# The last V block with two stationary quarters, and half a block of wo in eleven transfers of six partitions

## The chip, the core and the metric

The kernel runs on one core of a Trainium2 chip. The core has five engines with queues of their own: PE (TensorE, matrix products), DVE (VectorE), ACT (ScalarE), POOL (GpSimd) and SP (SyncE, which here only issues transfers). Data goes between the memory of the chip and the core's on-chip memory of 128 partitions by DMA, on 16 DMA engines that the core's queues share. The metric is the device time of one execution in microseconds (us).

## What is computed

One decoding step of a transformer layer for four sequences of one token each: layer norm, attention of 32 heads against a cache of 4096 keys and values, the output projection `wo`, a second layer norm, and a dense layer with the Mish activation. Cut to what matters:

```python
q = (layernorm(x) @ wq)                       # x: 4 x 1 x 640, 32 heads of 128
scores = einsum("bhqd,bhkd->bhqk", q, k_cache) * 128 ** -0.5
o = einsum("bhqk,bhkd->bhqd", softmax(scores), v_cache)   # 4096 keys for each head
h = x + o.reshape(B, Sq, H * Dh) @ wo
a = einsum("bsd,df->bsf", layernorm(h), w1) + b1          # 1728 wide
out = h + einsum("bsf,fd->bsd", a * tanh(softplus(a)), w2)
```

All inputs are bf16. The two caches are 134 MB each, and every byte of them is used once.

## The kernel before, in words

The work of the attention goes in 32 groups `g` (loop in line 427): one sequence and four heads each. For a group, one transfer brings 4 MB of K and one 4 MB of V; 32 KB lie on each partition, as 128 rows of 128 elements, 32 partitions to a head. Two buffers each hold K (`kt`) and V (`vt`).

- **Scores** (`mul_and_sum`, line 358): DVE multiplies K by the broadcast query in place (line 367), PE sums over the head dimension with an identity as the stationary operand (line 374), DVE reduces the rest (line 386), and ACT does the exponentials (line 417) into `e2`.
- **Values** (`pv_moving`, line 254): V passes through PE as the moving operand, 4 rows at a time, against 16 columns of weights, so that one matmul with 512 columns serves 4 rows. The products of four row indices lie beside one another in one PSUM bank; ACT copies the bank to `p_sb` (`pv_copy`, line 267), and four float32 matmuls collect the right pieces and add them up (`add_blocks`, line 273). They go to the profile as eight, as float32 takes two passes.
- **The last group** is cut finer: its K comes in two transfers, its V in four quarters of 32 rows each. Three quarters go through `pv_moving` (`R_LAST = R - R // VP`, line 521, which is 96 of 128 rows). The last goes through `pv_stationary` (line 284): each row of V is the stationary operand of a matmul with 4 columns, which adds straight into the result of `add_blocks`, with no copy.
- **The end**: `normalise` (line 307), the projection of the last four heads (`project`, line 348), the second layer norm, `w1` (line 563), Mish, `w2` (line 625), the sum and the store (line 649).

**The transfers** but one small one are issued by SP, in program order, and SP waits inside the queue until a buffer is free. Per group the order is: K of group g+2, V of group g+1, and in iterations 8 to 11 two blocks of `wo` (line 471), each of four heads (640 KB: 128 partitions with 5120 bytes each, the last block in pieces of 1280 bytes). Behind the last V stand, in this order, `w1` in two parts (line 502), `w2` in three parts (line 504) and the two rests of `w2`, `w2r_sb` and `w2s_sb` (lines 506 and 507). A transfer's completion is counted on one of eight semaphores in turn, so a transfer is also held until the one eight places ahead of it has landed. The projection of heads 20 to 23 stands in iteration 26 (`PROJ_AT`, line 227).

Of the kernel before, what the change touches and what calls it, by code (L numbers as in the profile page):

```python
# [16 lines left out]
def kernel(  # L17
# [24 lines left out]
    nc = tc.nc  # L42

    B, Sq, D = A_x.shape
    _, H, Sk, Dh = A_k_cache.shape
# [3 lines left out]
    G = 4  # L49
    PH = 128 // G  # L50
    R = Sk // PH
# [3 lines left out]
    HQ = H // G  # L55
# [7 lines left out]
    VP = 4  # L63
# [39 lines left out]
    def load_k(g):  # L103
        return load_kv(kpool, "kt", A_k_cache, g, NP)

    def load_v(g):
        return load_kv(vpool, "vt", A_v_cache, g, VP)
# [35 lines left out]
    for q in range(G):  # L143
        nc.vector.tensor_copy(
            out=sel[:, :, q, q * PH : (q + 1) * PH],
            in_=ident[0:N, 0:N].unsqueeze(2).to_broadcast([N, N, PH]),
# [81 lines left out]
    for hq in Q_AT[-1]:  # L228
# [12 lines left out]
        out=pick[:, :],  # L241
        in_=ident_f[:, :].rearrange("p (t i) -> p i t", t=T)[:, 0 : J * G, :],
# [11 lines left out]
    def pv_moving(g, r0, r1):  # L254
        for r in range(r0, r1, J):
            c0 = 128 // T * (r // J % T)
            nc.tensor.matmul(  # L257
                p_ps[c0 : c0 + J * G, :],
                lhsT=e2[g % NE2][:, r : r + J, :].rearrange("p j q -> p (j q)"),
                rhs=vts[g][:, r : r + J, :].rearrange("p j d -> p (j d)"),  # L260
                start=(r < J * T),
                stop=(r >= r1 - J * T),
            )

    def pv_copy(g):
        blocks[g] = work.tile([128, J * Dh], FP32, tag="p_sb", bufs=1, name=f"p_sb{g}")
        nc.scalar.copy(out=blocks[g][:, :], in_=p_ps[:, :])  # L267

    def add_blocks(g, stop=True):
        o = ot_of(g)  # L270
        p_sb = blocks.pop(g)
        for j in range(J):
            nc.tensor.matmul(  # L273
                o,
                lhsT=p_sb[:, j * Dh : (j + 1) * Dh],
                rhs=pick[:, j * G : (j + 1) * G],
                start=(j == 0),
                stop=(stop and j == J - 1),
            )
        return o  # L280
# [13 lines left out]
    def row_sums(hq):  # L294
        l_ps = ps.tile([128, N, G], FP32, tag="small")
        nc.tensor.matmul(  # L296
            l_ps[:, :, :],
            lhsT=ones_f[:, :],
            rhs=rs2[:, hq * N : (hq + 1) * N, :],
            start=True,  # L300
            stop=True,
        )
        rls[hq] = work.tile([128, N, G], FP32, tag="rl", name=f"rl{hq}")
        nc.vector.reciprocal(out=rls[hq][:, :, :], in_=l_ps[:, :, :])  # L304

    def normalise(hq):
        nc.vector.tensor_tensor(
            out=otn[:, hq, :, :],
            in0=ot.pop(hq)[:, :, :],
            in1=rls.pop(hq)[:, :, :],  # L310
            op=ALU.mult,
        )
# [15 lines left out]
    def regroup(hq):  # L328
        o4_ps = ps.tile([128, G, N], FP32, tag="small", name=f"o4_{hq}")
        for q in range(G):  # L330
            for i in range(G):
                nc.tensor.matmul(  # L332
                    o4_ps[q * PH : (q + 1) * PH, i, :],
                    lhsT=ident4[:, i, :],
                    rhs=otn[:, hq, :, q],
                    start=True,
                    stop=True,
                )
        nc.scalar.copy(out=o4[:, hq, :, :], in_=o4_ps[:, :, :])

    yT = ps.tile([128, DC, N], FP32, tag="yT")
    wo_sb = []

    def project(hq):

        for h in range(hq * G, (hq + 1) * G):
            for c in range(DC):
                nc.tensor.matmul(
                    yT[:, c, :],
                    lhsT=wo_sb[0][:, h, c * 128 : (c + 1) * 128],  # L350
                    rhs=o4[:, hq, h % G, :] if hq < HQ - 1 else otn[:, hq, :, h % G],
                    start=(h == 0 and c == 0),
                    stop=(h == H - 1 and c == DC - 1),
                )
# [3 lines left out]
    def mul_and_sum(g, part):  # L358

        hq, b = divmod(g, N)  # L360
        r0 = part * RP
        kt = kts[g][:, r0 : r0 + RP, :]
        s_ps = ps.tile([128, RP, W], FP32, tag="s", bufs=2, name=f"s{g}_{part}")
        s_of[g, part] = s_ps
        for k in range(NQ):
            d0 = k * DQ
            nc.vector.tensor_tensor(  # L367
                out=kt[:, :, d0 : d0 + DQ],
                in0=kt[:, :, d0 : d0 + DQ],
                in1=qbs[:, hq, b, d0 : d0 + DQ].unsqueeze(1).to_broadcast([128, RP, DQ]),  # L370
                op=ALU.mult,
            )
            for d in range(d0, d0 + DQ, W):
                nc.tensor.matmul(  # L374
                    s_ps[:, :, :],
                    lhsT=ident[:, :],
                    rhs=kt[:, :, d : d + W],
                    start=(d == 0),
                    stop=(d == Dh - W),
                )  # L380
            yield

    def finish_sum(g, part):
        if part == 0:
            s_sbs[g] = work.tile([128, R], FP32, tag="s_sb", name=f"s_sb{g}")
        nc.vector.tensor_reduce(  # L386
            out=s_sbs[g][:, part * RP : (part + 1) * RP],
            in_=s_of.pop((g, part))[:, :, :],
            axis=AX.X,
            op=ALU.add,  # L390
        )
# [35 lines left out]
    for g in range(NG):  # L427
        hq, b = divmod(g, N)
        for part in range(NP):
            now = mul_and_sum(g, part)  # L430
            before = None
            next(now)
            if part > 0:
                finish_sum(g, part - 1)
                if g >= 2:
                    add_blocks(g - 2)
                    if b == 1:
                        row_sums(hq - 1)
                        normalise(hq - 1)
                if g in PROJ_AT:  # L440
                    regroup(PROJ_AT[g])
            elif g >= 1:
                finish_sum(g - 1, NP - 1)
                before = softmax(g - 1)
                next(before)
            next(now)
            if before is not None:
                next(before)
        kts.pop(g)
        if g + 2 < NG:  # L450
            kts[g + 2] = load_k(g + 2)
        if 1 <= g < NG - 1:
            pv_moving(g - 1, 0, R)
            pv_copy(g - 1)
            vts.pop(g - 1)
        if g in PROJ_AT:
            project(PROJ_AT[g])
        if g + 1 < NG:
            vts[g + 1] = load_v(g + 1)
        for n in Q_AT.get(g, ()):  # L460
            q_chunk(n)
            q_broadcast(n)
        if g in WO_AT:

            if not wo_sb:
                wo_sb.append(wbig.tile([128, H, D], BF16, tag="w", name="wo_sb"))
            h0 = WO_AT[g] * WOC
            for h in range(h0, h0 + WOC, G):

                order = "(p i) n -> p i n" if h + G < H else "(i p) n -> p i n"  # L470
                nc.sync.dma_start(
                    out=wo_sb[0][:, h : h + G, :],
                    in_=A_wo[h * Dh : (h + G) * Dh, :].rearrange(order, i=G),
                )
            if WO_AT[g] == 0:
                nc.sync.dma_start(out=b1_row[:, :], in_=B_b1.rearrange("(o f) -> o f", o=1))
        if g == B1_AT:
            b_ps = ps.tile([128, FC], FP32, tag="small", name="b_ps")
            for c in range(FC):
                cols, fw = f_chunk(b1_row[:, :], c)  # L480
                nc.tensor.matmul(
                    b_ps[0:fw, c : c + 1],
                    lhsT=cols,
                    rhs=ident[0:1, 0:1],
                    start=True,
                    stop=True,
                )
            nc.vector.tensor_copy(out=b1T[:, 0:C2], in_=b_ps[:, 0:C2])
            nc.vector.tensor_copy(out=b1T[0:FREM, C2:FC], in_=b_ps[0:FREM, C2:FC])
# [28 lines left out]
    row_sums(HQ - 1)  # L518
    add_blocks(NG - 2)

    R_LAST = R - R // VP
    pv_moving(NG - 1, 0, R_LAST)
    pv_copy(NG - 1)
    pv_stationary(NG - 1, add_blocks(NG - 1, stop=False), R_LAST)
    normalise(HQ - 1)
# [20 lines left out]
    for dst in (h2T, hc):  # L546
        nc.vector.tensor_tensor(
            out=dst[:, :, :],
# [10 lines left out]
    for c0, c1 in W1_PARTS:  # L559
        for c in (0, C2, *range(1, C2)):  # L560
# [9 lines left out]
            if c0 == 0 and c == 4:  # L570
# [3 lines left out]
                    out=std[:, :], in_=v_ps[:, :], func=ACT.Sqrt, bias=eps_t[:, :], scale=1.0  # L574
# [5 lines left out]
        out=h1n[:, :, :],  # L580
# [6 lines left out]
        out=h1s[:, :, :],  # L587
# [9 lines left out]
        out=tb[:, :, :],  # L597
# [8 lines left out]
        out=ta[:, :, :], in0=tb[:, :, :], scalar1=-0.5, scalar2=-1.0, op0=ALU.mult, op1=ALU.add  # L606
# [4 lines left out]
        out=act_t[:, :, :],  # L611
# [10 lines left out]
    for i, (w2, c) in enumerate(w2_of):  # L622
        rows = 128 if c < C2 else FREM
# [10 lines left out]
        out=oT[:, :, :].rearrange("p n c -> p c n"),  # L634
# [46 lines left out]
```

## Time and profile before

| | |
|---|---|
| time, median of 3 runs | 667.99 us (667.97 to 668.5) |
| the profiled execution: its own time | 668.62 us |
| the profiled execution: span in the trace | 666.8 us |
| mean granted clock of PE | 0.837 |
| busy: PE, DVE, ACT | 444.7, 353.4, 115.0 us |
| read from the chip's memory | 283.35 MB, 425 GB/s over the span |
| packets of the transfers | 12,871 |

How to read it: the span goes from the first to the last instruction of one execution; its own time is 1.82 us longer and holds the start and the end around it. The page has a part for each question: busy time by engine, the span in 40 slices (the row DMA is the busy share of the 16 DMA engines, in tenths), the DMA queues, the chain that ended last (each piece of time put to what the next one waited for), the groups of instructions by line, and the transfers by line with their size and the median time from issue to landing. The trace behind it can be asked for the chain in order of time, for waits by engine, and for a timeline; it also has the start, length and size of every DMA packet, and the time of every completion count. A transfer adds one count for each DMA engine that has a share of it.

### The profile page before, as it was taken

To read this page: it belongs to the slowest core of one execution; us is meant where nothing else is said; L and a number is where in the kernel's file an instruction comes from. 1 tells how busy PE (TensorE), PEld (TensorE's weight loads), DVE (VectorE), ACT (ScalarE), POOL (GpSimd) and SP (SyncE) were. 2 spreads that over 40 slices of the span, in tenths; PEclk is the share of its full clock that TensorE was granted. 3 is DMA by queue.
4 is the path that set the end of the run, shared out by engine and by line. 5 is a ranking of instruction groups with operands and counts; after the bars stand their busy time and mean duration, and the time that the engine had idled before them with its cause. 6 is when DMAs were issued, how large, how long until landed. Compare 5 with 4: busy or idle time off the path is not lost.

```text
span 666.8 us, 7101 instructions
## 1 busy us (share of the span) xinstructions
PE 444.7 (67%) x3081; PEld 202.7 (30%) x3081; DVE 353.4 (53%) x306; ACT 115.0 (17%) x352; POOL 2.4 (0%) x13
## 2 busy tenths in 40 slices
PE   0588777887666485388666757757657785665876
PEld 0233333343222232133323323322223332222335
DVE  2485544566655366246654545656444666455732
ACT  0022122131101111011101111111011121011132
POOL 1000000000000000000000000000000000000000
PEclk9997889797779876777778898777798797779995
DMA  9999999999999999999999999999999999999996
GB/s 376 436 435 425 431 440 431 426 431 438 433 427 433 429 439 420 442 430 426 432 434 433 428 429 437 436 431 425 437 435 432 424 436 437 431 431 428 438 412 247
DMA packets 12871, 283.81 MB, mean 426 GB/s; under 512 B 1379, under 2 KB 2087, under 8 KB 4008
## 3 DMA queue, kind: packets, MB, share of 16 engines
q1 hardware_dynamic: 12832, 283.36, 98.9%
q8 instruction: 24, 0.39, 0.2%
q14 instruction: 7, 0.06, 0.0%
q10 hardware_dynamic: 8, 0.01, 0.0%
HBM read 283.35 MB, written 0.01 MB: 425 GB/s over the span
## 4 chain that ended last, share of the span: by engine, by line
DMA 62%; PE 21%; DVE 15%; issue 1%; ACT 0%; SPq 0%; DVEq 0%; ACTq 0%
DMA kt<-in_A_k_cache_dram 59%; PE s L374 16%; DVE kt L367 13%; DMA vt<-in_A_v_cache_dram 3%; DVE s_sb L386 1%; PE ot L273 1%; PE tr L399 1%; PE p_ps L257 1%; PE h_ps L563 0%; DVE mx L404 0%; PE q_ps L195 0%; PE y2T L625 0%; PE qb_ps L209 0%; PE tr L412 0%; PE o L332 0%
## 5 line engine op out<-in xcount | busy, mean ns | idle before, releaser
L374 PE MATMUL s<-kt,ident 128*128 128x512 bf16 x1024 | 300.0, 446 | 190.1 <-DVE kt L367 187.9
L367 DVE TENSOR_TENSOR kt<-kt,qbs 128x4096 bf16<-128x4096 bf16 x128 | 291.5, 2279 | 234.2 <-DMA kt<-in_A_k_cache_dram 234.2
L374 PEld LDWEIGHTS <-ident 128*128 128x128 bf16 x1024 | 109.4, 110 | 337.4 <-issue 170.6
L417 ACT ACTIVATE e<-s_sb,nbs 32x128 bf16<-32x128 f32 x128 | 74.0, 578 | 2.5
L257 PE MATMUL p_ps<-vt,e 128*16 128x512 bf16 x1016 | 63.4, 392 | 1.4 <-DMA vt<-in_A_v_cache_dram 1.4
L414 ACT COPY nbs<-tr 128x4 f32<-128x4 f32 x32 | 5.2, 162 | 332.0 <-PE tr L412 332.0
L386 DVE TENSOR_REDUCE s_sb<-s 128x64 f32<-128x512 f32 x64 | 43.6, 681 | 4.7 <-PE s L374 4.5
L267 ACT COPY p_sb<-p_ps 128x512 f32<-128x512 f32 x32 | 18.7, 585 | 151.8 <-PE p_ps L257 151.7
L273 PEld LDWEIGHTS ot<-pick,p_sb 128*128 128x128 f32 x256 | 34.3, 196 | 6.3 <-ACT p_sb L267 2.0
L257 PEld LDWEIGHTS <-e 128*16 128x16 bf16 x1016 | 23.0, 90 | 39.7 <-issue 19.0
L417 ACT ACTIVATION_READ_ACCUMULATOR e<-s_sb,nbs 32x1 f32 x128 | 32.2, 252 | 0.0
L273 PE MATMUL ot<-pick,p_sb 128*128 128x4 f32 x256 | 31.4, 246 | 1.0 <-ACT p_sb L267 1.0
L404 DVE TENSOR_REDUCE mx<-tr 1x4 f32<-1x128 f32 x32 | 8.9, 278 | 25.6 <-PE tr L399 25.5
L195 PE MATMUL q_ps<-wq_sb,xT 128*4 128x512 bf16 x40 | 11.0, 409 | 9.8 <-DMA wq_sb<-in_A_wq_dram 9.8
L399 PE MATMUL tr<-ident_f,pm 128*1 128x128 f32 x64 | 16.0, 345 | 1.2 <-DVE pm L397 1.2
L412 PEld LDWEIGHTS tr<-mx,nscale 1*128 1x128 f32 x64 | 9.4, 182 | 13.8 <-issue 11.4
L304 DVE RECIPROCAL rl<-l_ps 128x16 f32<-128x16 f32 x8 | 2.1, 258 | 20.3 <-PE l_ps L296 20.3
L209 PE MATMUL qb_ps<-q_all,sel 4*128 4x128 bf16 x128 | 9.2, 225 | 5.3 <-ACT q_all L202 5.3
L412 PE MATMUL tr<-mx,nscale 1*128 1x4 f32 x64 | 12.2, 258 | 0.4 <-DVE mx L404 0.4
L209 PEld LDWEIGHTS <-sel 4*128 4x128 bf16 x128 | 8.4, 98 | 9.1 <-issue 9.1
L202 ACT CAST q_all<-q_ps 4x512 bf16<-4x512 f32 x8 | 4.6, 574 | 35.0 <-PE q_ps L195 35.0
L399 PEld LDWEIGHTS tr<-ident_f,pm 128*1 128x1 f32 x64 | 2.8, 81 | 24.7 <-issue 24.7
(85 smaller groups left out, 75.2 us busy)
## 6 DMA issues: line engine op xcount, KB each, us to landing
kt<-in_A_k_cache_dram SPq DMA_DIRECT2D x31, 4096.0 KB, 25.1
vt<-in_A_v_cache_dram SPq DMA_DIRECT2D x31, 4096.0 KB, 33.3
wq_sb<-in_A_wq_dram SPq DMA_DIRECT2D x1, 5120.0 KB
wo_sb<-in_A_wo_dram SPq DMA_DIRECT2D x8, 640.0 KB, 35.6
kt<-in_A_k_cache_dram SPq DMA_DIRECT2D x2, 2048.0 KB
vt<-in_A_v_cache_dram SPq DMA_DIRECT2D x4, 1024.0 KB, 18.6
w<-in_B_w_dram SPq DMA_DIRECT2D x3, 640.0 KB, 17.8
w<-in_B_w_dram SPq DMA_DIRECT2D x1, 1296.0 KB, 25.3
```

What stands on the lines that cost most here:

```text
L195: nc.tensor.matmul(q_ps[:, :], lhsT=xT[:, c, :], rhs=wq_sb[:, c, n * QC : (n + 1) * QC], start=(c == 0), stop=(c == DC - 1),)
L209: nc.tensor.matmul(qb_ps[:, b * Dh : (b + 1) * Dh], lhsT=sel[:, b, q, :], rhs=q_all[:, h * Dh : (h + 1) * Dh], start=(q == 0), stop=(q == ...
L257: nc.tensor.matmul(p_ps[c0 : c0 + J * G, :], lhsT=e2[g % NE2][:, r : r + J, :].rearrange("p j q -> p (j q)"), rhs=vts[g][:, r : r + J, :]. ...
L267: nc.scalar.copy(out=blocks[g][:, :], in_=p_ps[:, :])
L273: nc.tensor.matmul(o, lhsT=p_sb[:, j * Dh : (j + 1) * Dh], rhs=pick[:, j * G : (j + 1) * G], start=(j == 0), stop=(stop and j == J - 1),)
L367: nc.vector.tensor_tensor(out=kt[:, :, d0 : d0 + DQ], in0=kt[:, :, d0 : d0 + DQ], in1=qbs[:, hq, b, d0 : d0 + DQ].unsqueeze(1).to_broadcas ...
L374: nc.tensor.matmul(s_ps[:, :, :], lhsT=ident[:, :], rhs=kt[:, :, d : d + W], start=(d == 0), stop=(d == Dh - W),)
L386: nc.vector.tensor_reduce(out=s_sbs[g][:, part * RP : (part + 1) * RP], in_=s_of.pop((g, part))[:, :, :], axis=AX.X, op=ALU.add,)
L399: nc.tensor.matmul(tr_ps[0:1, 0:128], lhsT=pm[:, :], rhs=ident_f[:, :], start=True, stop=True)
L404: nc.vector.tensor_reduce(out=mx[:, :], in_=tr_ps[0:1, 0:128].rearrange("o (a b) -> o a b", a=G), axis=AX.X, op=ALU.max,)
L412: nc.tensor.matmul(nb_ps, lhsT=nscale[:, :], rhs=mx[:, :], start=True, stop=True)
L417: nc.scalar.activation(out=e2[g % NE2][p0:p1, :, q], in_=s_sb[p0:p1, :], func=ACT.Exp, bias=nb[p0:p1, q : q + 1], scale=SCALE, accum_out=r ...
```

## The change

Two edits, independent of one another.

First, `R_LAST` goes from 96 to 64: of the last V, two quarters go through `pv_moving` and two through `pv_stationary`. That is 8 matmuls with 512 columns fewer, and 32 with 4 columns more.

Second, one of the eight blocks of `wo` (heads 20 to 23, `H_FEW` = 20) comes in twelve transfers in place of one. In iteration 10, where the whole block was issued, one transfer brings the even 64 partitions. The 64 odd ones follow in iterations 12 to 22, one transfer in each, as the last of its iteration: nine with six partitions and two with five, 22 partitions apart. The bytes are the same, and each lands in the same place.

```diff
+    H_FEW = H - 3 * G
+    FEW_AT = {HQ + 4 + i: i for i in range(11)}
+    few_rows = []
+
+    def load_few(p0, step, n):
+        part = slice(p0, p0 + step * (n - 1) + 1, step)
+        nc.sync.dma_start(
+            out=wo_sb[0][part, H_FEW : H_FEW + G, :], in_=few_rows[0][part, :, :]
+        )
...
-                nc.sync.dma_start(
-                    out=wo_sb[0][:, h : h + G, :],
-                    in_=A_wo[h * Dh : (h + G) * Dh, :].rearrange(order, i=G),
-                )
+                rows = A_wo[h * Dh : (h + G) * Dh, :].rearrange(order, i=G)
+                if h != H_FEW:
+                    nc.sync.dma_start(out=wo_sb[0][:, h : h + G, :], in_=rows)
+                else:
+                    few_rows.append(rows)
+                    load_few(0, 2, 64)
...
+        if g in FEW_AT:
+            load_few(1 + 2 * FEW_AT[g], 22, 6 if FEW_AT[g] < 9 else 5)
...
-    R_LAST = R - R // VP
+    R_LAST = R // 2
     pv_moving(NG - 1, 0, R_LAST)
     pv_copy(NG - 1)
     pv_stationary(NG - 1, add_blocks(NG - 1, stop=False), R_LAST)
```

## The prediction

> **What bounds the kernel now.** I read the DMA queues first, then the chain, then the chain in order of time at the end.
>
> ```profile
> DMA  9999999999999999999999999999999999999996
> ...
> q1 hardware_dynamic: 12832, 283.36, 98.9%
> q8 instruction: 24, 0.39, 0.2%
> q14 instruction: 7, 0.06, 0.0%
> ...
> DMA 62%; PE 21%; DVE 15%; issue 1%; ACT 0%; SPq 0%; DVEq 0%; ACTq 0%
> ```
>
> SP's queue fills the 16 DMA engines for 98.9% of the span. A compute edit inside the loop is worth nothing; only the bytes, how evenly they lie on the 16 engines, and what follows the last landing count. The chain's end:
>
> ```profile
> 628.77 20.61 DMA vt<-in_A_v_cache_dram
> 649.39 0.04 issue
> 649.43 1.05 PE p_ps L257 x7
> ...
> 650.56 0.59 ACT p_sb L267
> 651.15 0.04 issue
> 651.20 1.87 PE ot L273 x8
> 653.07 0.87 PE ot L284 x32
> 653.93 0.02 issue
> 653.95 0.18 DVE otn L307
> ...
> 661.58 2.20 PE y2T L625 x70
> ```
>
> The third V quarter lands at 649.38, then come its moving matmuls, the copy, eight passes of adding, and the stationary quarter. The fourth quarter is not in the chain: by its completion counts it landed at 651.89, 1.18 before PE took it up at 653.07.
>
> Now the balance. The counts of the last V quarter run from 647.11 to 651.89: the first DMA engine is done 4.78 us ahead of the last. On the first big load (wq) the spread was 1.37. By the packets every engine is equally fast, 1213 ns for 32 KB; what parts them is the other two queues. An instruction fetch starts, within 1 ns, where one engine's packet ends, and from then on that engine is later by 1.42 (16 KB fetches of q8; those of q14 cost 0.55 to 0.83). I followed the 16 engines by their completion times. The 24 fetches of q8 go round the same **eight** engines; with the last V these stand at 3.1 to 4.7 behind the first one. The other **eight** stand at 0, 0.4, 0.5, 0.7, 0.7, 1.3, 1.7 and 2.65. The last engine ends every transfer, so everything waits for it.
>
> **The small transfers.** The even half (64 partitions) still gives each engine 4 packets; the other 4 (196 ns long, 193 apart) go: -0.77 on every engine. Eleven transfers of six or five partitions give five engines 11 packets and a sixth 9, with a completion write each (199 ns for the pair): +2.19 and +1.79, net **+1.42** and +1.02.
>
> Which engines? The trace of before has no transfer of six. It has x_bf, with four partitions and four completions, and b_row, with one of each. b_row's packet follows the completion of the engine that stands at 0.36 (0.50 after it). Of x_bf's four, three completion writes are followed 6 ns later by the first wq packet of an engine, as in any chain of packets; all three are of the early eight, and b_row's is one of them. So small transfers use the same few engines, and these are early. I take it that those of six do too. In the late eight -0.77 brings 4.74 to 3.97. The worst early one goes from 2.65 to 4.07 if it is among the five. So the last landing moves by **-0.67 to -0.77**; I use -0.70. The bound on the other side is +1.42, if one of the latest engines is among the five.
>
> [...]
>
> SP issues eleven more transfers. wo's issues take 0.33 to 0.42 each, so 4 us in all, at the end of iterations in which SP then waits for a buffer:
>
> ```profile
> SPq L100 <- DVE kt L367: 469.5, 30, 34.1
> ```
>
> That is 15.7 us per wait, which hides them; without it, they would cost their 4 us. Their waits for a semaphore eight transfers back go some 50 us back (three transfers per iteration of 20 us), and a landing took 43 at most: no new wait. The rows are needed in iteration 26, the last comes in 22. PE's extra semaphore instruction (39 for 38) is nothing.
>
> **The second stationary quarter.** With the shift of -0.70, in the profiled execution's times:
> - K, the scores and the exponentials follow the landings, so the moving matmuls, 646.62 before, start at 645.9. The second quarter landed at 646.94, now 646.24; its 8 matmuls (1.05) end by about 647.4. Copy 0.59 and adding 1.87, with two gaps of 0.05: 649.95.
> - Third quarter: landed at 648.7, so its 32 stationary matmuls (0.87 in the chain, 0.99 from a standing start) run to 650.9.
> - Fourth quarter: lands at 651.19. PE waits 0.3, then 0.04 and 1.05 for 32 matmuls from a start: 652.28, for 653.93 before: **-1.65**. Of that 0.95 is this edit; the rest is the shift. It goes as the copy and the adding now lie under the transfers of the last two quarters.
>
> Behind the new wait of PE stand only the fourth quarter's matmuls, the normalising and the projection, which need it anyway. The eight moving matmuls saved had no cover; the 32 new ones lie before the last landing with 0.3 to spare (without that cover, up to 0.99).
>
> **What is late next.** The rest of the chain moves with it: w1's second part landed at 657.17 by its counts, and is needed at 658.4; both move, and 0.2 stays. Mish ends 1.65 earlier, and y2T starts at 659.93. Its last inputs:
>
> ```profile
> w2s_sb<-in_B_w_dram SPq DMA_DIRECT2D x1, 160.0 KB, 13.1
> w2r_sb<-in_B_w_dram SPq DMA_DIRECT2D x1, 80.0 KB, 14.8
> ```
>
> Issued at 649.40 and 647.45, they land at 662.5 and 662.2; w2's third part landed at 661.98. Before, y2T used the third part at 661.58 + 40 x 0.0314 = 662.84: spare. Now it comes to it at 661.19, and it lands at 661.28: +0.04, then 30 matmuls x 0.0314 = 662.26, for 663.78. So the end gains **1.5**, not 1.65: 668.62 - 1.5 = 667.1 for the profiled execution, 667.99 - 1.5 = **666.5** for the median. The profiled one lies 0.63 above the median; the gain is taken as the same.
>
> PE has 49 more instructions before the end, so its last fetch, at 662.73 while y2T ran, comes before y2T, while w2 still streams. In turn it falls on an engine at 3.50, then 3.50 - 0.77 + 1.42 = 4.15: 0.1 later than the 4.07 above.
>
> **The rivals.** What a measurement of this kernel can tell from no change is about 0.2%, 1.34 us.
> - *A, the forecast*: gain 1.2 to 1.8, 666.2 to 666.8. 0.58, of which 0.48 lies beyond 0.2%.
> - *B, the gain is cut at the end*: 666.8 to 667.4, likeliest 667.1. If the clock, which was at half from 647 on, is granted in full, adding takes 1.05 (as at 645.63) in place of 1.87 and the 8 matmuls half. Then before's own chain reaches the fourth quarter near 651.9, and the second edit is worth about 0.2, leaving 0.9. Or the last fetch delays w2 more. For it: the clock row of the page changes by the slice. 0.26.
> - *C, the six engines include a late one*: slower. The last landing moves by +1.42: fourth quarter 653.31, its matmuls done at 654.40 (+0.47); y2T starts at 662.05, w2's third part lands at 663.40, end 664.38 for 663.78: +0.6, **668.6**. It decides once a late engine of over 3.3 is among the five; from a shift of +0.8 the whole is a loss. Against it: the three marked engines. For it: no row has six. Range 667.9 to 668.8. 0.12.
> - *D, the transfers don't spread*: all 64 rows on one engine, 64 x 0.199 = 12.7, less 0.8: about 679 on a late engine. Against it: x_bf's four completions. 0.04.
>
> **The numbers.** Faster by over 0.2%: 0.48, from A. Within: 0.10 of A, B and C, 0.48. Slower: D, 0.04. The range is 666.0 to 667.9: A with the uncertainty of the clock and of the last engine, and B; it leaves out C, D and a little below, 0.2.
>
> **What would show it.** Completion counts of the last V spread over about 4.1 in place of 4.78, with the last count near 651.2; line 273 before the third quarter's landing; PE waiting for V ahead of the last 32 matmuls of line 284; and w2, not Mish, as y2T's last wait. Spread above 5.5 is C. Line 273 in under 1.1 us in a fast clock is B.

## The result, and the profile after

The changed kernel takes 670.83 us (median of 6, 670.65 to 672.94), the kernel before 668.56 beside it (667.97 to 668.78): ratio 1.0041, interval 1.0030 to 1.0052. It is slower, by 2.3 us. The forecast was 1.5 us faster. The profiled execution took 670.92 us, with a span of 669.1.

First the rows of the page that answer to those shown of before: the busy share of the DMA engines by slice, the queues (packets, MB, share of 16 engines), and the chain that ended last, by engine.

```profile
DMA  9999999999999999999999999999999999999995
...
q1 hardware_dynamic: 12896, 283.36, 98.8%
q8 instruction: 24, 0.39, 0.2%
q14 instruction: 7, 0.06, 0.0%
...
DMA 64%; PE 17%; DVE 17%; issue 1%; ACT 0%; SPq 0%; DVEq 0%
```

The bytes are the same, the 64 new packets are there, and the queue is as full as before. Nothing in these rows says that anything is wrong, yet this kernel needs 2.3 us more for the same bytes: 16 engines that are busy 98.8% of the time may still move fewer bytes while they are busy (424 GB/s in the mean of the span, 426 before). This is the trap of the case, and the reason why the packets' own lengths matter below.

The end of the chain, in order of time (start, length, what):

```profile
630.07 17.01 DMA vt<-in_A_v_cache_dram
647.08 0.02 issue
647.09 17.67 DMA w<-in_B_w_dram
664.76 0.05 issue
664.81 1.15 PE y2T L640 x30
```

Before, the chain went from V's third quarter through the adding, Mish and y2T. Now it goes from V's first quarter straight to the third part of w2, whose last count is at 664.76 (before: 661.98). Nothing that PE does with V sets the end any more.

PE at that time, from the timeline (start, busy, line, count, and in brackets the idle time ahead and what ended it):

```profile
649.16 1.05 PE L273 MATMUL ot<-pick,p_sb 128*128 128x4 f32 x8 [0.35 <-ACT p_sb L267]
650.14 1.04 PE L257 MATMUL p_ps<-vt,e 128*16 128x512 bf16 x16
651.93 1.87 PE L273 MATMUL ot<-pick,p_sb 128*128 128x4 f32 x8 [0.75 <-ACT p_sb L267]
653.66 1.87 PE L284 MATMUL ot<-e,vt 128*128 128x4 bf16 x64
...
663.22 1.21 PE L640 MATMUL y2T<-act_t,w 128*128 128x4 bf16 x40 [2.10 <-DVE act_t L625]
664.81 0.69 PE L640 MATMUL y2T<-act_t,w 128*128 128x4 bf16 x20 [0.39 <-DMA w<-in_B_w_dram]
```

The stationary quarters (line 284) now follow the adding (line 273), and y2T stops after 40 of its 70 matmuls for 0.39 us, for w2.

The completion counts, read from the trace (us; before, then after):

```
                          first count       last count        spread
last V, fourth quarter    647.11  648.26    651.89  654.46    4.78  6.20
w2, third part            657.13  658.22    661.98  664.76    4.85  6.54
```

Two things are to be seen. The first DMA engine to finish is 1.15 later, though ten of the 16 have 0.77 less to do than before. And the spread grew, where it was to shrink. The last landing of V moved by +2.57; -0.70 was forecast.

The packets' lengths say why the first engine is later. A 32 KB packet takes 1213 ns. In the changed kernel, around each small transfer but the first, 33 to 57 of the 32 KB packets are longer, most of them 1.23 to 1.33 us, from when the first engine passes it until the last one has. At its height every 32 KB packet that starts in 1.23 us is longer, 16 or more in a row, so all 16 engines are slowed. I call **excess** what packets of 1 to 32 KB take beyond the usual time of their size (1213 ns for 32 KB, 196 ns for 5 KB), summed over the engines; over 16 it is the mean delay per engine. Over the whole run it is 40.2 us, and 14.6 before (11.6 of it in 23 single long packets, most of them right behind an instruction fetch): 25.6 more, **1.6 us for each engine** in the mean.

### The profile page after: what moved, and what is told of

The parts are those of the page before. It is cut to its first block, busy times and chain, and to the rows that moved or that the text cites. A ratio compares the mean times of both kernels' runs of the same rounds, so it can differ in the third digit from the quotient of the medians.

```text
span 669.1 us, 7162 instructions
## 1 busy us (share of the span) xinstructions
PE 449.6 (67%) x3105; PEld 204.8 (31%) x3105; DVE 353.0 (53%) x306; ACT 114.9 (17%) x352; POOL 2.4 (0%) x13
## 3 DMA queue, kind: packets, MB, share of 16 engines
q1 hardware_dynamic: 12896, 283.36, 98.8%
## 4 chain that ended last, share of the span: by engine, by line
DMA 64%; PE 17%; DVE 17%; issue 1%; ACT 0%; SPq 0%; DVEq 0%
DMA kt<-in_A_k_cache_dram 59%; DVE kt L378 15%; PE s L385 14%; DMA w<-in_B_w_dram 3%; DMA vt<-in_A_v_cache_dram 3%; DVE s_sb L397 1%; PE tr L410 1%; PE ot L273 1%; PE p_ps L257 1%; DVE mx L415 1%; PE q_ps L195 0%; PE qb_ps L209 0%; PE o L332 0%; ACT q_all L202 0%; PE y2T L640 0%
## 5 line engine op out<-in xcount | busy, mean ns | idle before, releaser
L257 PE MATMUL p_ps<-vt,e 128*16 128x512 bf16 x1008 | 65.9, 407 | 0.0
```

Of the source, the lines that this page charges most:

```text
L257: nc.tensor.matmul(p_ps[c0 : c0 + J * G, :], lhsT=e2[g % NE2][:, r : r + J, :].rearrange("p j q -> p (j q)"), rhs=vts[g][:, r : r + J, :]. ...
```

## The experiments

Every time is the median of a kernel run beside the kernel before on the same chip; ratios are to that, with a 95% interval. Diffs are against the changed kernel if nothing else is said.

### Each edit alone

Stationary quarters alone: the kernel before with

```diff
-    R_LAST = R - R // VP
+    R_LAST = R // 2
```

> The second stationary quarter alone (R_LAST = R // 2, wo as before). Theory P: in the changed kernel this edit still gains about 1 us (the normalising at 655.56 stands 1.1 behind the last V landing at 654.46, before it stood 2.0 behind) and all of the loss is in the transfers; so this kernel takes 0.9 to 1.0 us off the kernel before, ratio 0.9985 to 0.9987, and its last V quarter lands within 0.2 of 651.9, with a spread near 4.8. Rival: the edit itself lengthens the end, by 24 more matmuls and an earlier instruction fetch; then it is at or above the time before.

668.20 (667.91 to 668.40), before 668.67: ratio 0.9993 [0.9983, 1.0002], so 0.47 ahead, too little to tell from no change. In its timeline:

```profile
651.92 1.01 PE L284 MATMUL ot<-e,vt 128*128 128x4 bf16 x32 [0.99 <-DMA vt<-in_A_v_cache_dram]
...
660.61 1.20 PE L625 MATMUL y2T<-act_t,w 128*128 128x4 bf16 x40 [2.10 <-DVE act_t L610]
662.17 0.69 PE L625 MATMUL y2T<-act_t,w 128*128 128x4 bf16 x20 [0.35 <-DMA w<-in_B_w_dram]
```

y2T starts 0.97 earlier than before (661.58), which is the 0.95 of the forecast. Then it waits 0.35 for w2, and the first of its last 30 matmuls comes at 662.17 where it was due at 661.58 + 40 x 0.0314 = 662.84 before: with the 1.15 that they take here against 0.94 before, 0.46 is left. Half of this edit's gain is cut off by a landing that it can't move.

The small transfers alone: `R_LAST` back to 96.

> The eleven small transfers alone, with three quarters of the last V moving as before. Theory (the small transfers cost every engine 1.6 us, and the sixth engine, which is one of the latest, 1.0 more; the stationary quarter is worth 0.5): 668.6 + 2.6 = 671.2, last V landing at 654.5, ratio 1.0035 to 1.0045. Rival (the two edits work against each other, as the earlier end of the last V only waits for w2): 670.8, as the changed kernel, ratio 1.0035 or less. As predicted before the change was run: 667.9.

670.90 (670.50 to 671.21), ratio 1.0034 [1.0022, 1.0047]. The interval allows both; the median is the rival's, the time of the changed kernel, and the timeline shows why the other edit adds nothing there:

```profile
662.90 1.20 PE L640 MATMUL y2T<-act_t,w 128*128 128x4 bf16 x40 [2.10 <-DVE act_t L625]
664.52 0.69 PE L640 MATMUL y2T<-act_t,w 128*128 128x4 bf16 x20 [0.42 <-DMA w<-in_B_w_dram]
```

With three moving quarters, too, y2T waits for w2. The whole loss is the small transfers'.

### Which engines, and where in the queue

Thirteen transfers of five partitions (the last of four), iterations 11 to 23, so that the sixth engine has none:

```diff
-    FEW_AT = {HQ + 4 + i: i for i in range(11)}
+    FEW_AT = {HQ + 3 + i: i for i in range(13)}
...
-            load_few(1 + 2 * FEW_AT[g], 22, 6 if FEW_AT[g] < 9 else 5)
+            load_few(1 + 2 * FEW_AT[g], 26, 5 if FEW_AT[g] < 12 else 4)
```

> The changed kernel with the odd rows in thirteen transfers of five partitions (the last of four), iterations 11 to 23, so that the sixth engine, which stood 3.3 behind at 311 us and 6.2 at the end, gets none. Theory P (two causes: the sixth engine is a late one, 1.0 us, and each small transfer slows all engines by about 0.15, 1.6 us in all): the spread at the end falls to 4.5 or less, the slow packets stay, last V landing about 653.4, time 0.7 to 1.2 us under the changed kernel. Rival (the late sixth engine is all of it): last V landing 651.2 and a time about 1.5 us below the kernel before.

669.74 (median of ten, of which one took 972.9), ratio 1.0016 [1.0006, 1.0025]: 1.1 under the changed kernel. The last V spreads over 4.99 in place of 6.20. The completion counts of the small transfers show the engine that is gone (behind the first count, iteration 14):

```
six partitions     0.0 0.5 1.2 1.2 1.8 3.4
five partitions    0.0 0.5 0.8 0.9 1.5
```

The sixth engine stands at 3.4, when the whole V spreads over 3.45: **it is one of the latest**. It gets 9 packets of the small transfers and loses 4, which is the +1.02 of the forecast, on the one engine on which it hurts. But the excess stays, at 24.6 us.

The small transfer behind K, ahead of V, in place of behind V:

```diff
+        if g in FEW_AT:
+            load_few(1 + 2 * FEW_AT[g], 22, 6 if FEW_AT[g] < 9 else 5)
         if 1 <= g < NG - 1:
...
-        if g in FEW_AT:
-            load_few(1 + 2 * FEW_AT[g], 22, 6 if FEW_AT[g] < 9 else 5)
```

> The changed kernel with each small transfer issued right behind K of its iteration, ahead of V, in place of right behind V. Theory P (the slowing goes with engines that skip a transfer, wherever it stands): the same slow packets, time within 0.5 us of the changed kernel. Rival (it goes with SP issuing the small one 0.4 us behind the V transfer; the first small transfer, held 7 us by a semaphore, had no slow packets): few slow packets, the last V landing 1.5 us earlier, time about 669.2.

670.71, ratio 1.0032 [1.0019, 1.0046]; excess 22.0. What stands beside it in the queue doesn't matter.

All 16 engines in each small transfer: four transfers of 16 partitions, 8 apart, iterations 12 to 15. In the traces of before and after, a transfer of 1, 4, 5, 6, 20, 64 or 128 partitions has 1, 4, 5, 6, 10, 16 or 16 completion writes; that 16 partitions go to 16 engines is my estimate from these.

```diff
-    FEW_AT = {HQ + 4 + i: i for i in range(11)}
+    FEW_AT = {HQ + 4 + i: i for i in range(4)}
...
-            load_few(1 + 2 * FEW_AT[g], 22, 6 if FEW_AT[g] < 9 else 5)
+            load_few(1 + 2 * FEW_AT[g], 8, 16)
```

> The changed kernel with the 64 odd rows in four transfers of 16 partitions, one packet for each engine (iterations 12 to 15), in place of eleven of six. Theory P (the slow packets of 1240 to 1330 ns come when a transfer runs on some of the engines only): no slow packets, last V landing as before within 0.2, time equal to that of the stationary quarter alone within 0.3 us. Rival (any small transfer behind a V does it): slow packets at four places, about 0.17 us each, 0.7 in all, on every engine.

670.64, ratio 1.0030 [1.0019, 1.0041]; 5.0, 7.9, 8.8 and 9.1 us of excess. My theory then (P, that the slowing comes from leaving some engines out) fell: with all engines alike it is worse for each transfer.

### When, and how many

Thirteen of five again, right behind the transfers of wo (`FEW_AT = {8: (0, 1, 2), 9: (3, 4, 5), 10: (6, 7, 8), 11: (9, 10, 11, 12)}`):

> The 64 odd rows go in thirteen transfers of five partitions (the last of four), three each in iterations 8 to 10 and four in iteration 11, right behind the transfers of wo; the two stationary quarters stay. Theory S (a small transfer slows every engine's packets while it passes, about 1.9 us of packet time for each, wherever it stands): 13 x 1.9 / 16 = 1.5 us for each engine, 669.7 us as with one in each iteration from 11 on, ratio 1.0015. Rival L (only those from iteration 13 on slow the others, as the earliest one or two in each run so far did not): packet excess below 3 us in all, the late engines keep their -0.77 or most of it, the last V lands 0.3 to 0.8 ahead of the kernel with the stationary edit alone: 667.4 to 668.0, ratio 0.998 to 0.999.

670.00, ratio 1.0021 [1.0011, 1.0030]; the excess is 34.8 over that of before, where S had 25. And seven in iteration 16, six in iteration 17 (`FEW_AT = {16: range(0, 7), 17: range(7, 13)}`):

> The same thirteen transfers of five, but seven one behind another in iteration 16 and six in iteration 17, with the two stationary quarters. Theory S (paid by each transfer): excess 13 x 1.9 = 25 us, 669.7 us, ratio 1.0015. Rival O (paid once for each occasion at which the engines go from one large transfer to the next past small ones): two occasions, excess about 5 us, 0.3 us for each engine, so 668.3 to 668.7. Rival L (late ones only): as S.

673.29, ratio 1.0071 [1.0054, 1.0087]; 29.6 more excess. So the price is paid by each transfer, wherever it stands: L (only late ones slow the others) and O (paid once for each occasion) fell. The time of this one holds a second cost. A transfer waits in SP for the one eight places ahead of it (9.0 us for one of V and 9.0 for one of K at the small transfers), so the next K came too late, and the queue ran dry; the row for 380 to 390 us (span's length, busy times, clock, DMA share, GB/s) shows the only stretch of the loop that is far from full, a share of 0.64:

```profile
core 0: us, PE busy (x) PEld busy (x) DVE busy (x) ACT busy (x) POOL busy (x), PEclk, DMA share, GB/s
370.00:380.00 10.00, 5.39 (x83) 3.15 (x83) 4.14 (x4) 0.77 (x4) 0.00 (x0) 1.00 1.00 428
380.00:390.00 10.00, 9.05 (x39) 4.01 (x39) 9.23 (x8) 2.48 (x9) 0.00 (x0) 0.83 0.64 260
```

That is 3.6 us of 10 without work.

### The size of a transfer

The odd half in one transfer of 64 partitions, 2 apart, in iteration 16 (`FEW_AT = {16: 0}`, `load_few(1, 2, 64)`):

> The 64 odd rows go in one transfer of 64 partitions in iteration 16, four packets for each engine, with the two stationary quarters: no rebalancing at all. If the slowing comes from transfers with one packet for an engine (theory S): no excess, the time of the stationary edit alone, 668.2 us, ratio 0.999 to 1.000. If any transfer of 5 KB rows put between two large ones after the projections have begun does it (rival L): excess 2 to 8 us, 0.1 to 0.5 us for each engine, 668.3 to 668.7.

668.30, ratio 0.9995 [0.9985, 1.0004]; excess 0.0. In two transfers of 32, 4 apart, in iterations 13 and 14, two packets for each engine by the same estimate (`load_few(1 + 2 * FEW_AT[g], 4, 32)`):

> [...] Rival S (it is the single packet): none or little excess, 668.3. A cost that falls with the packets for each engine (none at four, 7.9 us at one for 16 engines): 1 to 4 us for each transfer, 668.3 to 668.7. A cost of any transfer that is shorter than the engines' spread of 3 us: 8 us each, 1 us for each engine, 669.2. [...]

668.35, ratio 0.9997 [0.9987, 1.0006]; excess 0.0. Splitting a block in these two ways costs nothing. By then two theories were alive: S, now narrowed to "a single packet for an engine slows", and W, "a packet in another engine's partitions slows", where whose partitions they are was an assumption.

### The place

The same sizes in other places. The halves as the lower and the upper 64 partitions, iterations 10 and 16 (`load_few(0, 1, 64)`, `load_few(64, 1, 64)`):

> The block goes as the lower 64 partitions in iteration 10 and the upper 64 in iteration 16, each side by side, four packets for each engine; the two stationary quarters stay. [...] Theory W (what slows is an engine writing into another's partitions: each such packet costs about its own 0.196 us to others): 128 x 0.196 = 25 us of packet time, 1.6 for each engine, 669.5 to 669.9, ratio 1.0015. Rival S (only transfers with one packet for an engine slow): no excess, 668.3, ratio 0.9995.

672.35, ratio 1.0059 [1.0044, 1.0074]. Not a packet more than in the run with the halves 2 apart, and 4.0 us slower. 28.5 and 44.3 us of excess stand around the two halves, where W had 25 for both and S none. The rows of the stretch in which the second half passes, first here, then in the run with one transfer 2 apart:

```profile
core 0: us, PE busy (x) PEld busy (x) DVE busy (x) ACT busy (x) POOL busy (x), PEclk, DMA share, GB/s
388.00:394.00 6.00, 5.87 (x47) 3.26 (x50) 3.12 (x3) 2.49 (x9) 0.00 (x0) 1.00 1.00 286
```

```profile
core 0: us, PE busy (x) PEld busy (x) DVE busy (x) ACT busy (x) POOL busy (x), PEclk, DMA share, GB/s
385.00:391.00 6.00, 5.69 (x34) 3.02 (x35) 3.96 (x3) 2.50 (x9) 0.00 (x0) 1.00 1.05 453
```

Both are fully busy; the one moves 286 GB/s, the other 453 (a packet is counted where it starts, so a share can pass 1: 453 / 1.05 = 431).

Sixteen partitions side by side, 64 + 16i, iterations 13 to 16, the first half being the lower 64 (`load_few(64 + 16 * FEW_AT[g], 1, 16)`):

> The even and odd halves become the lower and the upper 64 partitions; the upper 64 go in four transfers of 16 partitions that lie side by side, in iterations 13 to 16, with the two stationary quarters. One packet for each of the 16 engines, as in the run with 16 partitions 8 apart, which had 29 us of excess and 670.6. If the slowing comes from the partitions lying apart, and so in other engines' places (rival W): no excess, 668.2. If it comes from the small transfer as such (theory S): the same 29 us, 670.6, ratio 1.003.

672.68, ratio 1.0060 [1.0045, 1.0075]; 9.5 to 9.9 us for each of the four, and 21.0 for the lower 64. W as it was put here, with only partitions that lie apart in other engines' places, failed: 39 us where it had none. But the lower 64, with four packets for each engine, slowed too, which S does not explain. So W could be kept only with another assumption on which partitions are whose, and no run shows whose they are.

Transfers of 78, 25 and 25 partitions; from the same counts I estimate 13 engines with six packets for the 78, and five with five for each 25, so eight packets more on five engines (`load_few(50, 1, 78)`, then `load_few(0, 1, 25)` and `load_few(25, 1, 25)`). This was the attempt at the gain that the change sought, without single packets:

> The block goes as 78 partitions (13 engines, six packets each) in iteration 10 and 25 and 25 (five engines, five packets each) in iterations 12 and 14, with the two stationary quarters: no engine has a single packet, the first five get eight packets more than before (+1.54 us), the next eight two less (-0.39), the last three eight less (-1.54). Rival S (only single packets slow): no excess, the late engines gain 0.39, 667.7 to 668.0, the best so far. Theory W (writing into another engine's partitions costs others as much as it takes): some 20 us of excess, 1.2 for each engine, 668.9 to 669.5, so that bytes cannot be moved away from a late engine this way.

672.42, ratio 1.0059 [1.0044, 1.0074]; 37.4, 11.9 and 19.7 us of excess. S failed, as by that estimate no engine had a single packet; W had an excess, but 20 us where 69 came.

Eights, 8 apart, by turns in the lower and the upper half of the partitions (iterations 13 to 20):

> The odd half goes in eight transfers of eight partitions, 8 apart, in iterations 13 to 20, by turns in the lower and the upper half of the partitions, with the two stationary quarters. [...] Theory W: the transfers in the upper half show 8 x 0.196 = 1.6 us more of excess than those in the lower half. Rival S: all alike, by one packet each some 0.2 to 0.5 us for each of the eight, 2 to 4 us a transfer. The time is not decisive: sixth to eighth engine get 1.0 more, 669.5 to 671.5.

671.02, ratio 1.0042 [1.0025, 1.0059]. Excess of the lower ones 1.3, 4.3, 1.9, 1.9, of the upper ones 4.4, 5.1, 5.0, 4.8. The place matters: the upper ones have 2.5 us more in the mean, where W had 1.6. But the lower ones are not free, and one of them costs nearly as much as the upper ones.

What tells S from W in one run is the same with 4 in place of 8 between the partitions (`FEW_AT` gives the first partition, 1, 65, 3, 67, 33, 97, 35, 99; `load_few(FEW_AT[g], 4, 8)`):

> The odd half goes in eight transfers of eight partitions 4 apart, in iterations 13 to 20, by turns in the lower and the upper 64 partitions, with the two stationary quarters. The first eight engines carry all of it, one packet each per transfer, 8 in all (net +0.8 on these, -0.77 on the others). [...] Theory W (only a packet in another engine's place slows): the four lower transfers show no excess (under 0.3 us each), the four upper 4 to 6 us each, as the upper ones of the run with 8 apart; 20 us in all, 1.2 for each engine. Rival S (a single packet for an engine slows wherever it goes): lower ones 1.3 us and more, as with 8 apart. Time 669.5 to 671.0. [...]

670.01, ratio 1.0025 [1.0016, 1.0034]. The stretches around the eight transfers, lower and upper by turns:

```profile
core 0: us, PE busy (x) PEld busy (x) DVE busy (x) ACT busy (x) POOL busy (x), PEclk, DMA share, GB/s
327.00:331.00 4.00, 4.00 (x18) 1.83 (x17) 3.98 (x3) 1.54 (x6) 0.00 (x0) 0.90 0.96 415
346.50:350.50 4.00, 3.58 (x22) 2.07 (x19) 4.00 (x3) 2.49 (x9) 0.00 (x0) 1.00 0.98 400
366.00:370.00 4.00, 3.57 (x17) 1.65 (x16) 3.05 (x3) 1.83 (x7) 0.00 (x0) 1.00 0.99 427
385.50:389.50 4.00, 3.93 (x20) 1.93 (x18) 4.00 (x3) 1.76 (x7) 0.00 (x0) 0.96 1.01 410
405.50:409.50 4.00, 3.93 (x18) 1.76 (x18) 3.85 (x4) 1.30 (x5) 0.00 (x0) 0.90 1.03 438
425.00:429.00 4.00, 4.00 (x16) 1.67 (x16) 3.57 (x4) 0.80 (x4) 0.00 (x0) 0.78 1.03 417
444.50:448.50 4.00, 3.58 (x18) 1.74 (x18) 3.08 (x3) 1.72 (x7) 0.00 (x0) 1.00 0.97 419
464.50:468.50 4.00, 3.73 (x21) 1.91 (x18) 4.00 (x3) 2.04 (x8) 0.00 (x0) 1.00 1.04 424
```

GB/s over the DMA share is the rate while busy: 432, 408, 431, 406, 425, 405, 432, 408. By the packets' lengths, the excess:

```
iteration     13   14   15   16   17   18   19   20
partitions    low  up   low  up   low  up   low  up
excess, us    0.0  4.1  0.0  4.1  0.5  4.2  0.0  3.9
```

The 0.5 of iteration 17 is one long packet at 407 us, which stands there in the kernel before too. Eight single packets each, the same place in the queue, and only the upper ones slow: **the place decides**, as W had put it in numbers (none, and 4 to 6 us), and S fell. Two packets for each engine in the place in which single ones were slow (two blocks of wo halved, the odd rows of both in four transfers of 16 partitions 8 apart):

```diff
-            out=wo_sb[0][part, H_FEW : H_FEW + G, :], in_=few_rows[0][part, :, :]
+            out=wo_sb[0][part, H_FEW - G : H_FEW + G, :].rearrange(
+                "p (b i) n -> p b i n", b=2
+            ),
+            in_=A_wo[(H_FEW - G) * Dh : (H_FEW + G) * Dh, :].rearrange(
+                "(b p i) n -> p b i n", b=2, i=G
+            )[part],
...
+            load_few(1 + 2 * FEW_AT[g], 8, 16)
```

> Two blocks of wo (heads 16 to 19 and 20 to 23) are halved; the odd rows of both go together in four transfers of 16 partitions 8 apart, in iterations 13 to 16, so each engine gets two packets for one partition, with the two stationary quarters. Rival S (the single packet slows): no excess, as with 32 partitions, 668.3, ratio 0.9995. Theory W (the place, which is the same as in the run with 16 partitions and one packet, 7.9 us each): twice as many misplaced packets, 10 to 16 us of excess each, 40 to 64 in all, 2.5 to 4 for each engine, 670.8 to 672.3, ratio 1.004 to 1.006.

673.50, ratio 1.0073 [1.0058, 1.0088]; 16.8, 17.5, 17.5 and 20.1 us, twice what single packets cost there. The place again: 71.9 us in all, above the 40 to 64 that W had put. Which engine carried which row, the trace doesn't tell, here or in any run.

### What the bytes were worth, and one thing left open

The small transfers left out, the odd partitions of that block set to zero by GpSimd (`FEW_AT = {}` and a memset ahead of the even half):

> The eleven small transfers are left out, and with them half of one block of wo: the 64 odd partitions of that block are set to zero by GpSimd instead, so this part of the projection is missing. What is left is what the small transfers were to buy: every engine has four packets of 5 KB less (-0.77 us), none has more, and nothing is misplaced. The two stationary quarters stay. Theory: the last V and w2 land 0.77 ahead of the kernel with the stationary edit alone, 667.4 to 667.6, ratio 0.998, no packet excess: the term of -0.77 was sized right and is the most that such a change can gain. Rival (a late engine's bytes do not set the landing): 668.2, ratio 0.9993.

667.50 (667.00 to 668.41), ratio 0.9983 [0.9974, 0.9992]. The last V landed at 651.17, 0.71 ahead of the kernel with the stationary quarters alone (651.88), with no more excess than before. So the -0.77 was sized right.

The changed kernel's small transfers in the reverse order:

> The changed kernel with its eleven small transfers in the reverse order: the one with partitions 1, 23, 45, 67, 89, 111, which showed no excess in iteration 12, goes last, in iteration 22, and the one that showed 2.2 us there goes first. If the freedom belongs to the place (these partitions): 2 us or more of excess in iteration 12, none in iteration 22. If it belongs to the time (the first one behind wo): none in iteration 12, 2 us in iteration 22. The time is that of the changed kernel, 670.5 to 671.2.

670.85, ratio 1.0031 [1.0019, 1.0043]; 0.1 us of excess in iteration 12, 1.7 in iteration 22. The freedom belongs to the time, not to the place. It held for every transfer of six or five in iteration 12 (and one in iteration 11), but not for sixteen in iteration 12 (5.0) nor for those in the runs behind wo. Why, I can't say.

## Why the prediction was wrong

**The step that failed** is the sum over the late engines: "In the late eight -0.77 brings 4.74 to 3.97 ... So the last landing moves by -0.67 to -0.77". The -0.77 itself is right, as the run without the small transfers shows (-0.71). Two terms are missing from it, and the last V landed 2.57 later instead:

- *The price of a small transfer's packet to the other engines.* The sum gave a packet the time that its own engine spends on it, 0.199, and nothing to the others. By the runs, the large packets get longer (the small ones hardly: a median of 196 to 209 ns in each small transfer of the changed kernel), and the lag reaches all 16. With the excess over that of before divided by the 64 packets of the odd half, the price is 0.40 us (changed kernel), 0.38 (fives), 0.49 (sixteens), 0.54 (fives behind wo), and 0.51 for the upper eights (16.3 / 32): **two to three times the packet's own 0.196**, paid by all together. It is no constant: the other runs lie between 0.16 (the cheapest of the lower eights, 8 apart) and 0.79 (the last 25), and the same lower 64 cost 28.5 us in one run and 21.0 in another. So 64 packets cost 25.6 / 16 = 1.6 on an engine in the mean and gain 0.77 on the late ones.
- *The sixth engine.* The forecast had its +1.02 but put that engine in the wrong place: three of the first four were seen to be early (x_bf), and I took the sixth to be so too. It is among the latest, and by these terms it lands its last V 1.02 + 1.6 = 2.6 later than before; the last landing moved by 2.57. The run with fives, 1.1 us faster, has the excess without that term.

That the place decides is shown. For each transfer, the excess was 0.0 us with 64 rows 2 apart, with 32 rows 4 apart and, but for one packet that is long in the kernel before too, with eight rows 4 apart in the lower half; 3.9 to 4.2 with eight rows 4 apart in the upper half; 1.3 to 4.3 and 4.4 to 5.1 with eight rows 8 apart in the lower and the upper half; 5.0 to 9.1 with sixteen rows 8 apart, and 9.5 to 9.9 with sixteen side by side.

Why it decides is not shown. That a packet slows the others where it goes into partitions that another engine writes (W) was my assumption: no trace has a packet's engine or partition. What W put for the halves and for the two runs of eights counts on whose partitions they are; no run shows that, and in its place the runs show the excess by place, 28.5 and 44.3 us for the halves and the figures above for the eights. And in every run a row's place in the chip's memory goes with its partition, so that no run tells a slowing where the engines write from one where they read.

The other steps:

- *b_row*, the one transfer of a single packet in the full queue of before (3.4 KB in 135 ns), shows no price to the other engines: it passed at 221 us, and no 32 KB or 5 KB packet around it is longer. But by the runs there are places that cost nothing, so it can't stand for eleven transfers, whose price came to 1.6 us for each engine.
- *Rival C* (a late engine among the six) was right in its mechanism, at 0.12, and gave 668.6; its sign, a spread above 5.5, came with 6.20. It was sized without the first term, so the result lies 2.2 above it.
- *The issues of SP* were hidden, as forecast, but longer than forecast: 0.70 to 0.73 each where 0.33 to 0.42 were put, and 6.48 for the first, where no new wait was forecast. All eleven took 13.6 us, not 4, and SP's wait for K's buffer takes them up (457.0 for 469.5, 12.5 us less):

```profile
271.22 6.48 SPq L350 DMA_DIRECT2D wo_sb<-in_A_wo_dram  x1
...
299.24 0.71 SPq L350 DMA_DIRECT2D wo_sb<-in_A_wo_dram  x1
```

```profile
SPq L100 <- DVE kt L378: 457.0, 30, 34.6
```

- *The stationary quarter* is worth 0.97 at the start of y2T, as forecast (0.95), but the forecast counted on w2 landing 0.70 earlier. With w2 where it was, 0.47 is left; with w2 later, nothing.
- *What is late next*: w2 and not Mish, right in the changed kernel and with the stationary quarters alone, but not always. In the profiled execution of the run without the small transfers, the slowest of its eleven (668.41), the clock stood at 0.50 from 646 us on (0.83 in the mean from 646 to 650 with the stationary quarters alone), and y2T ran through without a wait for w2 (line 273 took 1.87 us at 645.69, and 1.05 at 645.62 with the stationary quarters alone).
- *w1's second part* landed at 657.12 by its counts, not at 657.17; nothing rests on the difference.

No kernel with all the work beats the one with the stationary quarters alone, and its own 0.47 can't be told from no change. Whether a late engine can be relieved in this way at all is not shown.

## What to carry to other kernels

A DMA queue that is "99% busy" says nothing about the rate (286 and 453 GB/s here, both fully busy): look at how long a packet of one size takes over time, and suspect a change that makes packets longer, not only one that adds some. When all engines stream, try in which partitions a small transfer is free: 64 rows 2 apart and 32 rows 4 apart were here (0.0 us of excess), and runs of neighbours (44.3 us for the upper 64), rows 8 apart (5.0 to 9.1 for sixteen), 22 apart (25.6 for eleven transfers) or 26 apart (24.6 for thirteen), and eight rows 4 apart in the upper half (3.9 to 4.2) were paid by all 16. Before bytes are moved to "early" engines, find where each of these stands, and ask whether the resource that is late is the engine at all.

## What the runs showed of the hardware

- A transfer of six 5 KB packets, 22 partitions apart, lengthened the 32 KB packets of all engines for about 4 us, from 1213 ns to mostly 1.23 to 1.33 us; one of sixteen, 8 apart, to up to 1.64 us.
- 64 rows of 5 KB in one transfer cost 0.0 us of excess 2 partitions apart (the odd ones) and 44.3 us side by side (the upper 64).
- An instruction fetch of 16 KB puts one engine back by some 1.4 us (about 0.93 for itself, 0.5 in the packet behind it), and nothing in the loop gives it back: with the last V of the kernel before the engines lie 4.8 us apart, though all but 37 of its 9216 packets of 32 KB and 5 KB are equally long to 15 ns.
- Eleven small transfers, one in each iteration, took 13.6 us of SP's time out of its waits; seven in a row held SP for 23 us, and 3.6 us of the queue stood empty.
